# Cosine attention and a gated feed-forward on one core: other load order, batch 2 prepared beside the first output, first output tile ahead of each gate step, loads on the SP queue

## The chip, the cores and the metric

The kernel runs on one core of a Trainium2 chip. The core has a matrix engine (PE; its weight loads are listed as PEld), a vector engine (DVE), an activation engine (ACT), a general engine (POOL) and a queue engine (SP) that only starts transfers. Each engine works through its own list of instructions in order and waits on semaphores. Transfers started by SP go through a hardware queue, those started by POOL through a software queue; both use the same 16 DMA engines. The metric is the device time of one execution in microseconds; the kernel before took 351.66 us, the median of 13 runs (349.85 to 354.13).

## The reference

```
q, k, v: 8 batches x 8 heads x 576 positions x 64, float32
phi(x) = concat(relu(x) * cos(theta_s), relu(x) * sin(theta_s))     theta_s = pi/2 * s / 576
kv  = phi(k)^T v  per batch and head;   z = sum over s of phi(k)
attn = (phi(q) kv) / (phi(q) z + 1e-6)
x   = attn, heads side by side: 4608 tokens x 512
xn  = x / sqrt(mean(x*x) + 1e-6) * rms_g
out = (silu(xn w_gate) * (xn w_val)) w_out        d_ff = 1536
```

The attention is linear: per batch there is one small matrix kv (with z beside it) and a product with it for each position.

## The kernel before, in words

**Tiles.** Of a batch's 576 positions 512 are "main", four tiles (j = 0 to 3) of 128 positions. The other 64 are the rest; the rests of two batches make one more tile (index 4, `NJ`), which is worked on with the odd batch of the pair. The feed-forward goes by blocks of 512 tokens: blocks 0 to 7 are the mains of batches 0 to 7, block 8 holds all rests. d_ff is cut into 12 columns of 128 (`NNT`), so a block has 12 gate steps.

**Attention of one batch b.** `k_prep` (L154) makes phi(k) with two scaled relus, cosine and sine half; `v_prep` (L163) casts v; `kvz` (L217) multiplies them on PE, 40 small matmuls, and `kvz_out` (L231) copies the result to SBUF. `q_scale` (L178) makes phi(q) and `q_tr` (L184) transposes it by a DMA on SP, or `q_tr_pe` and `q_out` do so on PE with a copy. Then, per tile, `nd` (L241): eight matmuls for numerators and denominators; `x_of` (L260): three DVE instructions (den, rec, xt), a Square with a sum on ACT (scr) and a power on POOL (rs); `xn_scale` (L290): the RMS norm on DVE; and the transpose of the result into xnT, by PE and an ACT copy (`xn_tr_pe`, `xn_out`) for batches 0 to 2, by a DMA on SP (`xn_tr`) later. `nd` and `kvz` use one PSUM buffer (pool "att", one deep).

**Feed-forward of one block.** A gate step (`gval`, L351) is eight matmuls 512 wide into two PSUM tiles (four with w_gate, four with w_val), a Silu on ACT (sil) and a product on DVE (hT). Each of the two PSUM tiles has two buffers, so gate step n needs that hT of step n - 2 is done. `outp(blk, i, n)` (L374) does n of the block's 48 output matmuls (four tiles of 12); a tile's last one is followed by `store`: a copy on ACT and a transfer by SP.

**Order.** The order is written out by hand, the same for all engines. Batch 0 comes first. Then gate block 0 (loop at L600) with batch 1's q and k prepared between its steps; then the output of block 0 as a stage of its own (loop at L621, four matmuls a step, all four tiles at once in the PSUM buffers of the gate), with the attention of batch 1 between. From block 1 on (loop at L647) each gate step of block blk is followed by four output matmuls of block blk - 1 (none in block 1), with the next batches' attention around it: `before(b, r)` is what is issued ahead of the gate step, `after(b, r)` what follows, where r counts the gate steps of block b - 1: r = 0 is its first step, negative r lie in block b - 2. Which piece goes to which r stands in `PLAN`, and in `PLAN_2` and `PLAN_3` for batches 2 and 3. After block 8 the output of block 8 follows as the tail.

**Loads.** q, k and v of batch 0 go through SP, everything else through POOL's queue: the six weight pieces of `load_wgv` (512 columns of w_gate and of w_val each), batch 1, `load_wout`, batch 2; from batch 3 on `loads_of` (L510) issues pieces between the gate steps, also on POOL. `raw` tiles have six buffers, taken in the order of the loads: a batch uses those of the batch two before. POOL also computes rs, in the same in-order list. DMAs that POOL or SP issue share eight semaphores per queue in turn, so that a DMA is issued only when the one eight before it has landed.

Of the kernel before, what the change touches and what calls it, by code (L numbers as in the profile page):

```python
# [17 lines left out]
def kernel(  # L18
# [14 lines left out]
    nc = tc.nc  # L33
# [57 lines left out]
    raws = {}  # L91

# [21 lines left out]
    def load(what, src, b):  # L114
        load_piece(what, src, b, 0, H, nc.gpsimd)
        if b % 2 == 0:
            load_rest(what, src, b, nc.gpsimd)
            load_rest(what, src, b + 1, nc.gpsimd)
# [281 lines left out]
    for s in range(0, DFF, 512):  # L400
        load_wgv(s)
# [137 lines left out]
    def plans(t, **pre):  # L539
# [16 lines left out]
    def before(b, r):  # L556
# [4 lines left out]
        for what, n in PLANS.get(b, PLAN)[0].get(r, ()):  # L561
            if n == NJ and what != "v" and b % 2 == (what in ("q", "k")):
                continue
            if what == "q":
                if n == NJ:
                    qr_prep(b)
                else:
                    q_scale(b, n, V, sin_eng)
                    q_tr(b, n)
            elif what == "k":  # L570
                k_prep(b, n, V, sin_eng)
            elif what == "v":
                v_prep(b, n)
            elif what == "kvz_out":
                kvz_out(b, 0, A)
                kvz_out(b, 1, V)
            elif what == "x":
# [5 lines left out]
        if b == 2 and 8 <= r <= 11:  # L583
            xn_out(2, r - 8)

    def after(b, r):
# [3 lines left out]
        for what, n in PLANS.get(b, PLAN)[1].get(r, ()):  # L590
            if what == "kvz":
                kvz(b, 0, H)
            elif n < NJ or b % 2 == 1:
                nd(b, n)
        if b == 2 and 7 <= r <= 10:
            xn_tr_pe(2, r - 7)
# [3 lines left out]
    for nn in range(2, NNT):  # L600
        if 8 <= nn <= 11:
            q_out(1, nn - 8, V if nn % 2 else A)
        if 6 <= nn <= 9:
            q_scale(1, nn - 6, V, A)
        if nn == 9:
            k_prep(1, 0, V, A)
        if nn == 10:
            k_prep(1, 1, V, A)
            qr_prep(0)
        if nn == 11:  # L610
            k_prep(1, 2, V, A)
            k_prep(1, 3, V, A)
        gval(0, nn)
        if 7 <= nn <= 10:
            q_tr_pe(1, nn - 7)
    k_prep(1, NJ, V, A)
    for c in range(NJ + 1):
        v_prep(1, c, A if c % 2 else V)
    for j in range(NJ):
        accs[0, j] = pools["gv"].tile([P, DM], FP32, name="acc", tag="gv"[j % 2])  # L620
    for nn in range(NNT):  # L621
        if nn == 2:
            kvz_out(1, 0, A)
            kvz_out(1, 1, V)
        if 3 <= nn <= 6:
            x_of(1, nn - 3)
        if 5 <= nn <= 8:
            xn_scale(1, nn - 5)
        if 7 <= nn <= 10:
            xn_out(1, nn - 7)  # L630
        for j in range(NJ):
            nc.tensor.matmul(  # L632
                accs[0, j][:, :], lhsT=hTs[0][:, nn, j * P : (j + 1) * P], rhs=wo[:, nn, :],
                start=(nn == 0), stop=(nn == NNT - 1),
            )
        if nn == 1:
            kvz(1, 0, H)
        if 2 <= nn <= 5:
            nd(1, nn - 2)
        if 6 <= nn <= 9:  # L640
            xn_tr_pe(1, nn - 6)
    for j in range(NJ):
        store(0, j, accs[0, j])

    for blk in range(1, NBLK):  # L647
        for nn in range(NNT):
# [49 lines left out]
```

## Time and profile before

| what | us |
|---|---|
| median of 13 runs | 351.66 |
| the profiled execution's own time | 352.21 |
| its span, first to last instruction | 350.4 |
| PE busy | 319.8 |
| DVE, ACT, POOL busy | 193.6, 154.2, 90.9 |

The span cut into 40 slices, with each engine's busy share in tenths, the granted PE clock and the DMA engines:

```profile
PE   1559998988799997999999999999999999999993
DVE  4764475555697795479547974783573322222200
ACT  4634592794545435244534363553443233232221
PEclk9999999999999998999999999999999999999998
DMA  7899999391597999449998999892022001100023
```

A slice is 8.76 us. The first slices are the prologue with batch 0. Gate block 0 ends at 51.6 us, the output of block 0 at 68.2, gate block 1 at 99.5, gate block 2 at 136.2; the tail begins at 333.9. Busy time of PE is counted from the start of a matmul to its modelled end, so groups with a gap between them count 0.17 us more than those without.

### The profile page before, as it was taken

How to read it: one execution, taken by the hardware profiler on the slowest of the kernel's cores; microseconds unless marked ns; L12 is line 12 of the kernel's file. 1: busy time of each engine (PE TensorE's matmuls, PEld its weight loads, DVE VectorE, ACT ScalarE, POOL GpSimd, SP SyncE). 2: the span in 40 equal slices, each digit the busy share in tenths (PEclk: the TensorE clock that was granted, in tenths of full speed). 3: DMA queues.
4: the chain of work that ended last, by engine and by line, in shares of the span. 5: the costliest groups of instructions: out<-in, count | busy, mean ns of one | idle time of the engine just before them, and what ended most of it. 6: DMA issues, size and time to landing. Idle time of an engine off the chain costs nothing.

```text
span 350.4 us, 5676 instructions
## 1 busy us (share of the span) xinstructions
PE 319.8 (91%) x2096; PEld 160.6 (46%) x2096; DVE 193.6 (55%) x419; ACT 154.2 (44%) x304; POOL 90.9 (26%) x135
## 2 busy tenths in 40 slices
PE   1559998988799997999999999999999999999993
PEld 1448454434345543554454445445544444444441
DVE  4764475555697795479547974783573322222200
ACT  4634592794545435244534363553443233232221
POOL 0527622401414572048015711510110000000000
PEclk9999999999999998999999999999999999999998
DMA  7899999391597999449998999892022001100023
GB/s 241 214 206 290 326 303 283 123 278 24 179 181 144 214 183 290 121 103 211 215 101 225 229 173 220 159 257 60 33 74 62 30 30 53 39 30 32 32 60 91
DMA packets 64477, 53.59 MB, mean 153 GB/s; under 512 B 45953, under 2 KB 53633, under 8 KB 64449
## 3 DMA queue, kind: packets, MB, share of 16 engines
q1 hardware_dynamic: 52304, 23.60, 32.7%
q0 software_dynamic: 12144, 29.63, 32.1%
q8 instruction: 16, 0.26, 0.3%
q14 instruction: 13, 0.10, 0.1%
HBM read 38.01 MB, written 9.44 MB: 135 GB/s over the span
## 4 chain that ended last, share of the span: by engine, by line
PE 77%; DVE 8%; ACT 6%; DMA 4%; issue 2%; POOL 0%; SPq 0%; ACTq 0%; DVEq 0%
PE gps L340 23%; PE vps L340 23%; PE acc L377 22%; PE kvz L225 3%; PE nd L254 3%; DVE xt L272 2%; DMA raw<-in_v_dram 2%; DVE hT L349 2%; PE tps L196 1%; ACT sil L348 1%; PE acc L632 1%; DMA raw<-in_q_dram 1%; DMA remk<-in_k_dram 1%; DVE kp L141 1%; ACT scr L280 1%
## 5 line engine op out<-in xcount | busy, mean ns | idle before, releaser
L349 DVE TENSOR_TENSOR hT<-vps,sil 128x512 bf16<-128x512 f32 x108 | 74.4, 690 | 113.8 <-PE vps L340 73.6
L340 PE MATMUL gps<-xnT,wg 128*128 128x512 bf16 (+1 forms) x456 | 113.5, 373 | 2.6 <-ACT sil L348 2.5
L340 PE MATMUL vps<-xnT,wv 128*128 128x512 bf16 (+1 forms) x456 | 113.8, 373 | 0.0
L377 PE MATMUL acc<-wo,hT 128*128 128x512 bf16 x384 | 97.0, 380 | 0.0
L348 ACT ACTIVATE sil<-gps 128x512 bf16<-128x512 f32 x108 | 63.9, 593 | 61.3 <-PE gps L340 58.8
L340 PEld LDWEIGHTS <-wv 128*128 128x128 bf16 x456 | 44.7, 100 | 50.7 <-issue 1.1
L340 PEld LDWEIGHTS <-wg 128*128 128x128 bf16 x456 | 42.1, 100 | 43.9 <-issue 3.6
L285 POOL TENSOR_TENSOR rs<-ssq,mhalf 128x1 f32<-128x1 f32 x36 | 20.5, 570 | 148.3 <-ACT scr L280 148.3
L377 PEld LDWEIGHTS <-hT 128*128 128x128 bf16 x384 | 37.7, 98 | 46.0 <-issue 1.1
L280 ACT ACTIVATE scr<-xt 128x513 bf16<-128x513 f32 x36 | 22.9, 635 | 59.6 <-DVE xt L272 59.6
L359 ACT COPY osb<-acc 128x512 f32<-128x512 f32 x36 | 20.7, 586 | 28.8 <-PE acc L377 28.3
L293 DVE SCALAR_TENSOR_TENSOR xn<-xt,rs,gb 128x512 bf16<-128x512 f32 x36 | 26.7, 743 | 1.3 <-POOL rs L285 1.3
L272 DVE TENSOR_TENSOR xt<-nd,rec 128x512 f32<-128x512 f32 x36 | 24.9, 692 | 1.2
L148 ACT CAST vv<-raw 128x512 bf16<-128x512 f32 x28 | 15.9, 621 | 14.6 <-DMA raw<-in_v_dram 14.6
L254 PE MATMUL nd<-kvzs,qpT 128*128 128x65 bf16 x256 | 14.3, 200 | 5.9 <-DVE xt L272 5.4
L254 PEld LDWEIGHTS <-qpT 128*128 128x128 bf16 x256 | 12.4, 102 | 14.9 <-DVE xt L272 6.2
L141 DVE TENSOR_SCALAR qp<-raw,cos_tab 128x512 bf16<-128x512 f32 x32 | 16.2, 517 | 3.6 <-DMA raw<-in_q_dram 3.6
L225 PE MATMUL kvz<-vv,kp 128*128 128x65 bf16 x256 | 12.4, 199 | 4.7 <-DVE vv L150 3.2
L225 PEld LDWEIGHTS <-kp 128*128 128x128 bf16 x320 | 12.0, 101 | 8.9 <-ACT kp L139 3.4
L97 POOL DMA_DIRECT2D raw<-in_k_dram x20 | 15.3, 764 | 2.6 <-DMA raw<-in_v_dram 2.1
L97 POOL DMA_DIRECT2D raw<-in_v_dram x20 | 15.3, 765 | 2.2 <-DVE qp L141 2.2
L97 POOL DMA_DIRECT2D raw<-in_q_dram x20 | 15.7, 788 | 0.2 <-issue 0.2
(64 smaller groups left out, 190.4 us busy)
## 6 DMA issues: line engine op xcount, KB each, us to landing
out_dram<-osb SPq DMA_DIRECT2D x32, 256.0 KB, 3.2
raw<-in_q_dram POOLq DMA_DIRECT2D x16, 256.0 KB, 7.8
raw<-in_k_dram POOLq DMA_DIRECT2D x16, 256.0 KB, 4.0
raw<-in_v_dram POOLq DMA_DIRECT2D x16, 256.0 KB, 4.9
raw<-in_q_dram POOLq DMA_DIRECT2D x2, 1024.0 KB, 11.2
raw<-in_k_dram POOLq DMA_DIRECT2D x2, 1024.0 KB, 11.1
raw<-in_v_dram POOLq DMA_DIRECT2D x2, 1024.0 KB, 10.7
wg<-in_moe_w_gate_dram POOLq DMA_DIRECT2D x3, 512.0 KB, 9.0
```

The lines of the kernel that those rows point to most:

```text
L97: eng.dma_start(out=raws[what, b][:, h0 : h0 + n, :], in_=src[b, h0 : h0 + n, 0:SM, :].rearrange("h (p j) d -> p h (j d)", j=NJ),)
L225: nc.tensor.matmul(kvz_ps[b][:, h // 2 % 2, c0 : c0 + DE], lhsT=kp[:, c, h, :], rhs=vv[:, c, h, :] if c < NJ else vvr[:, b % 2, h, :], sta ...
L254: nc.tensor.matmul(ps[rows, h // HH, (h % HH) * DE : (h % HH + 1) * DE], lhsT=src[:, h, cols], rhs=kz[:, h, :], start=True, stop=True,)
L272: nc.vector.tensor_tensor(out=xt[:, 0:DM].rearrange("p (g h d) -> p g h d", g=2, d=D), in0=ndv[:, :, :, 0:D], in1=rec[:, :].rearrange("p ( ...
L280: nc.scalar.activation(out=scr[:, :], in_=xt[:, :], func=AF.Square, scale=DM**-0.5, accum_out=ssq[:, :],)
L285: nc.gpsimd.tensor_tensor(out=rs[:, :], in0=ssq[:, :], in1=mhalf[:, :], op=ALU.pow)
L293: nc.vector.scalar_tensor_tensor(out=t[:, :], in0=xt[:, 0:DM], scalar=rs[:, 0:1], in1=gb[:, :], op0=ALU.mult, op1=ALU.mult,)
L340: nc.tensor.matmul(ps[:, c0 : c0 + n], lhsT=w[:, dt, nn * P : (nn + 1) * P], rhs=xnTs[blk][:, dt, c0 : c0 + n], start=(dt == 0), stop=(dt ...
L348: nc.scalar.activation(out=sil[:, :], in_=gps[:, :], func=AF.Silu)
L349: nc.vector.tensor_tensor(out=hTs[blk][:, nn, :], in0=vps[:, :], in1=sil[:, :], op=ALU.mult)
L359: nc.scalar.copy(out=osb[:, :], in_=acc[:, :])
L377: nc.tensor.matmul(acc[:, :], lhsT=hTs[blk][:, nn, j * P : (j + 1) * P], rhs=wo[:, nn, :], start=(nn == 0), stop=(nn == NNT - 1),)
```

## The change

It has five parts.

1. Loads at the start: q and k of batch 1 are put on POOL's queue ahead of the last third of the gate and value weights; after those come v of batch 1, the rests, and w_out's thirds with batch 2's k, v and q between them. `load` becomes `load_first`.
2. Batch 1 is prepared earlier in gate block 0: its q from step 3, its k and v complete before the block's end, and `kvz(1)` ahead of the output of block 0.
3. The output of block 0: its first 8 columns for all tiles at once as before, then the last 4 columns tile by tile, so that the tiles end one after another, with copies by ACT and DVE in turn. The attention of batch 1 takes every second step. Batch 2's k is prepared here, and the rest of batch 2 is spread over block 1 with one tile per two gate steps. Its fourth tile is finished in block 2.
4. From block 2 on, the first output tile (12 matmuls; in block 2, 18) comes ahead of the block's first gate step, and the others are spread over the 12 steps.
5. q, k and v loads from batch 3 on are issued by SP, two gate steps earlier from batch 4 on; the plans of batch 3 (one step later) and of v (from r = -1) are shifted.

```diff
-    def load(what, src, b):
-        load_piece(what, src, b, 0, H, nc.gpsimd)
-        if b % 2 == 0:
-            load_rest(what, src, b, nc.gpsimd)
-            load_rest(what, src, b + 1, nc.gpsimd)
+    def load_first(what, b):
+        load_piece(what, srcs[what], b, 0, H, nc.gpsimd)
+        if b == 2:
+            load_rest(what, srcs[what], 2, nc.gpsimd)
+            load_rest(what, srcs[what], 3, nc.gpsimd)
...
-    def store(blk, j, acc):
+    def store(blk, j, acc, eng=nc.scalar):
         osb = osb_pool.tile([P, DM], FP32, name="osb", tag="osb")
-        nc.scalar.copy(out=osb[:, :], in_=acc[:, :])
+        copy(eng, osb[:, :], acc[:, :])
...
-    for s in range(0, DFF, 512):
-        load_wgv(s)
+    load_wgv(0)
+    load_wgv(512)
+    load_first("q", 1)
+    load_first("k", 1)
...
-    for what, src in (("q", q), ("k", k), ("v", v)):
-        load(what, src, 1)
-        if what == "q":
-            load_rest(what, src, 0, nc.gpsimd)
-        load_rest(what, src, 1, nc.gpsimd)
-    for s in range(3):
-        load_wout(s)
-    for what, src in (("q", q), ("k", k), ("v", v)):
-        load(what, src, 2)
+    load_wgv(1024)
+    load_rest("k", k, 1, nc.gpsimd)
+    load_first("v", 1)
+    load_rest("v", v, 1, nc.gpsimd)
+    load_rest("q", q, 0, nc.gpsimd)
+    load_rest("q", q, 1, nc.gpsimd)
+    load_wout(0)
+    load_first("k", 2)
+    load_wout(1)
+    load_first("v", 2)
+    load_wout(2)
+    load_first("q", 2)
...
-        first, cut = {2: (None, 1), 3: (-9, 2)}.get(b, (-14, 4))
+        first, cut = {2: (None, 1), 3: (-9, 2)}.get(b, (-16, 4))
...
-        load_piece(what, src, b, n * e, n, nc.gpsimd)
+        load_piece(what, src, b, n * e, n, nc.sync)
         if e == cut - 1 and b % 2 == 0:
-            load_rest(what, src, b, nc.gpsimd)
-            load_rest(what, src, b + 1, nc.gpsimd)
+            load_rest(what, src, b, nc.sync)
+            load_rest(what, src, b + 1, nc.sync)
...
     PLAN = plans(
-        1, q=each(-5, 5), k=each(-3, 5), v=((-2, (0, 1)), (-1, (2, 3)), (0, (4,))),
+        1, q=each(-5, 5), k=each(-3, 5), v=((-1, (0, 1)), (0, (2, 3, 4))),
     )
     PLAN_3 = plans(
-        2, q=each(-2, 5), k=((-1, (0,)), (0, (1, 2)), (1, (3,)), (2, (4,))),
-        v=((0, (0, 1)), (1, (2, 3)), (2, (4,))),
-    )
-    PLAN_2 = plans(
-        4, q=((0, (0, 1)), (1, (2, 3))), k=((2, (0, 1)), (3, (2, 3)), (4, (4,))),
-        v=((2, (0, 1)), (3, (2, 3)), (4, (4,))),
+        3, q=each(0, 4), k=((0, (0, 1)), (1, (2,)), (2, (3,))),
+        v=((1, (0, 1)), (2, (2, 3, 4))),
+    )
+    PLAN_2 = plan_of(
+        k=[(-9, (0,)), (-7, (1,)), (-5, (2,)), (-3, (3,)), (-1, (4,))],
+        v=[(0, range(NJ + 1))], kvz_out=[(2, (0,))],
+        q=[(2, (0, 1)), (3, (2, 3))],
+        x=[(5, (0,)), (7, (1,)), (9, (2,)), (11, (3,))],
+        xn=[(6, (0,)), (8, (1,)), (10, (2,))],
+        xn_out=[(8, (0,)), (10, (1,))],
+    ), plan_of(
+        kvz=[(1, (0,))], nd=[(4, (0,)), (6, (1,)), (8, (2,)), (10, (3,))],
+        xn_tr=[(7, (0,)), (9, (1,)), (11, (2,))],
     )
...
     for nn in range(2, NNT):
-        if 8 <= nn <= 11:
-            q_out(1, nn - 8, V if nn % 2 else A)
+        if 5 <= nn <= 8:
+            q_out(1, nn - 5, V if nn % 2 else A)
+        if 3 <= nn <= 6:
+            q_scale(1, nn - 3, V, A)
         if 6 <= nn <= 9:
-            q_scale(1, nn - 6, V, A)
+            k_prep(1, nn - 6, V, A)
         if nn == 9:
-            k_prep(1, 0, V, A)
+            k_prep(1, NJ, V, A)
         if nn == 10:
-            k_prep(1, 1, V, A)
-            qr_prep(0)
+            v_prep(1, 0, A)
+            v_prep(1, 1, V)
+            v_prep(1, 2, A)
         if nn == 11:
-            k_prep(1, 2, V, A)
-            k_prep(1, 3, V, A)
+            v_prep(1, 3, V)
+            v_prep(1, NJ, V)
         gval(0, nn)
...
+    kvz(1, 0, H)
...
-        for j in range(NJ):
+        if nn == 11:
+            qr_prep(0)
+        if nn in (5, 7, 9, 11):
+            xn_out(1, nn // 2 - 2)
+        before(2, nn - 12)
+        for j, m in ((j, nn) if nn < 8 else (nn - 8, 8 + j) for j in range(NJ)):
...
+        if nn >= 8:
+            store(0, nn - 8, accs[0, nn - 8], V if nn % 2 else A)
...
+            if blk == 2 and nn == 0:
+                xn_scale(2, 3)
+                xn_out(2, 2)
             for b, r in ahead:
                 before(b, r)
+            first = {1: 0, 2: NNT + 6}.get(blk, NNT)
+            if blk >= 2 and nn == 0:
+                outp(blk - 1, 0, NNT)
+                if blk == 2:
+                    xn_tr_pe(2, 3)
+                    xn_out(2, 3)
+                outp(blk - 1, NNT, first - NNT)
             gval_mm(blk, nn, 0, SM)
             gval_end(blk, nn)
             if blk >= 2:
-                outp(blk - 1, 4 * nn, 4)
+                i, e = (first + (NJ * NNT - first) * m // NNT for m in (nn, nn + 1))
+                outp(blk - 1, i, e - i)
```

More of the change, by code (lines that the diff above doesn't have):

```diff
@@ L91 @@
     raws = {}
+    srcs = {"q": q, "k": k, "v": v}
     def load_piece(what, src, b, h0, n, eng):
@@ L572, in before @@
             elif what == "v":
-                v_prep(b, n)
+                v_prep(b, n, V if b == 2 and n % 2 else A)
             elif what == "kvz_out":
@@ L576, in before @@
                 kvz_out(b, 1, V)
+            elif what == "xn_out":
+                xn_out(b, n)
             elif what == "x":
@@ L582, in before @@
                 xn(b, n)
-        if b == 2 and 8 <= r <= 11:
-            xn_out(2, r - 8)
     def after(b, r):
@@ L592, in after @@
                 kvz(b, 0, H)
+            elif what == "xn_tr":
+                xn_tr_pe(b, n)
             elif n < NJ or b % 2 == 1:
                 nd(b, n)
-        if b == 2 and 7 <= r <= 10:
-            xn_tr_pe(2, r - 7)
     for nn in range(2, NNT):
-        if 8 <= nn <= 11:
-            q_out(1, nn - 8, V if nn % 2 else A)
+        if 5 <= nn <= 8:
+            q_out(1, nn - 5, V if nn % 2 else A)
+        if 3 <= nn <= 6:
+            q_scale(1, nn - 3, V, A)
         if 6 <= nn <= 9:
-            q_scale(1, nn - 6, V, A)
+            k_prep(1, nn - 6, V, A)
         if nn == 9:
-            k_prep(1, 0, V, A)
+            k_prep(1, NJ, V, A)
         if nn == 10:
-            k_prep(1, 1, V, A)
-            qr_prep(0)
+            v_prep(1, 0, A)
+            v_prep(1, 1, V)
+            v_prep(1, 2, A)
         if nn == 11:
-            k_prep(1, 2, V, A)
-            k_prep(1, 3, V, A)
+            v_prep(1, 3, V)
+            v_prep(1, NJ, V)
         gval(0, nn)
[L614 to L618, printed above, removed]
+        if 4 <= nn <= 7:
+            q_tr_pe(1, nn - 4)
+    kvz(1, 0, H)
     for j in range(NJ):
@@ L621 @@
     for nn in range(NNT):
-        if nn == 2:
+        if nn == 0:
             kvz_out(1, 0, A)
             kvz_out(1, 1, V)
[L625 to L630, printed above, removed]
-        for j in range(NJ):
+        if nn in (1, 3, 5, 7):
+            x_of(1, nn // 2)
+        if nn in (4, 6, 8, 10):
+            xn_scale(1, nn // 2 - 2)
+        if nn == 11:
[4 more added lines that the diff above has]
+        for j, m in ((j, nn) if nn < 8 else (nn - 8, 8 + j) for j in range(NJ)):
             nc.tensor.matmul(
-                accs[0, j][:, :], lhsT=hTs[0][:, nn, j * P : (j + 1) * P], rhs=wo[:, nn, :],
-                start=(nn == 0), stop=(nn == NNT - 1),
-            )
[L636 to L643, printed above, removed]
+                accs[0, j][:, :], lhsT=hTs[0][:, m, j * P : (j + 1) * P], rhs=wo[:, m, :],
+                start=(m == 0), stop=(m == NNT - 1),
+            )
+        if nn >= 8:
+            store(0, nn - 8, accs[0, nn - 8], V if nn % 2 else A)
+        if nn in (0, 2, 4, 6):
+            nd(1, nn // 2)
+        if nn in (4, 6, 8, 10):
+            xn_tr_pe(1, nn // 2 - 2)
     for blk in range(1, NBLK):
```

## The prediction

> **What bounds the kernel now.** I read the page first, then PE's busy time stage by stage, then PE's list of waits, and last the timelines of the places that this list names.
>
> ```profile
> span 350.4 us, 5676 instructions
> PE 319.8 (91%) x2096; PEld 160.6 (46%) x2096; DVE 193.6 (55%) x419; ACT 154.2 (44%) x304; POOL 90.9 (26%) x135
> ```
>
> PE is the bound, and the instruction lists of both kernels hold the same 4194 rows for PE: only PE's idle and slow time can go. The stages below are the stage of output 0 (with batch 1), gate block 1 (with batch 2), gate block 2 (with batch 3), the first step of block 3, and the rest up to the last output.
>
> ```profile
> 51.59:68.16 16.57, 14.82 (x138) 7.55 (x137) 10.86 (x26) 7.81 (x19) 6.51 (x8) 1.00 0.63 191
> 68.16:99.46 31.30, 25.50 (x185) 12.32 (x184) 18.64 (x39) 20.96 (x43) 6.75 (x10) 1.00 0.61 180
> 99.46:136.19 36.73, 34.77 (x250) 17.13 (x249) 28.25 (x64) 15.65 (x35) 18.18 (x26) 1.00 0.95 192
> 136.19:140.46 4.27, 4.27 (x12) 1.59 (x12) 4.27 (x10) 3.05 (x6) 0.00 (x0) 0.60 1.11 293
> 140.46:333.88 193.42, 193.42 (x1170) 92.80 (x1169) 101.82 (x200) 75.34 (x149) 37.16 (x55) 1.00 0.52 112
> ```
>
> Columns: stretch, its length, busy us of PE, PEld, DVE, ACT, POOL, granted clock, DMA share, GB/s. From 140.46 on PE has no gap: nothing can be gained there, only lost. The prologue (0 to 32.5 us) and the tail keep their order. So the whole case is the stretch 51.6 to 140.5. Who makes PE wait in it:
>
> ```profile
> PE gps L340 <- ACT sil L348: 2.5, 2, 2.0
> PE nd L254 <- DVE xt L272: 2.4, 5, 0.9
> PE tpx L314 <- DVE xn L293: 2.0, 3, 1.4
> PE kvz L225 <- ACT vvr L170: 1.5, 1, 1.5
> ```
>
> The waits on xt and xn are one loop through the in-order engines:
>
> ```profile
> 90.81 0.64 ACT L280 ACTIVATE scr<-xt 128x513 bf16<-128x513 f32 x1 [1.88 <-DVE xt L272]
> 91.91 0.60 ACT L348 ACTIVATE sil<-gps 128x512 bf16<-128x512 f32 x1
> 92.54 0.69 DVE L349 TENSOR_TENSOR hT<-vps,sil 128x512 bf16<-128x512 f32 x1 [1.18 <-ACT sil L348]
> 93.58 0.69 DVE L272 TENSOR_TENSOR xt<-nd,rec 128x512 f32<-128x512 f32 x1
> 94.19 0.74 DVE L293 SCALAR_TENSOR_TENSOR xn<-xt,rs,gb 128x512 bf16<-128x512 f32 x1
> 94.99 0.40 PE L314 MATMUL tpx<-ident,xn 128*128 128x128 bf16 x4 [1.45 <-DVE xn L293]
> ```
>
> The Square (scr) of one tile stands ahead of the gate's Silu on ACT, hT behind that on DVE, the next xt behind hT, and PE's transpose behind xn: 3.1 us a round (scr at 87.73, then 90.81), while PE has 2.2 us of work in it. The 2.0 us wait on sil is a load:
>
> ```profile
> 127.35 0.60 ACT L348 ACTIVATE sil<-gps 128x512 bf16<-128x512 f32 x1
> 134.50 1.14 ACT L148 CAST vv<-raw 128x512 bf16<-128x512 f32 x2 [6.55 <-DMA raw<-in_v_dram]
> 135.55 0.59 ACT L348 ACTIVATE sil<-gps 128x512 bf16<-128x512 f32 x1
> ```
>
> ACT stands 6.55 us on batch 4's v pieces with a Silu queued behind; PE idles 1.96 us and then runs at half clock.
>
> **What the Trainium skill says.** "TensorE: Matmul & The Clock Gate", Part 1 (the HAM clock gate): a low-activity window of about 3.4 us halves PE's clock. The trace agrees on the length (0.5 for 3.41 us from 136.61) but shows that 1.96 us of idling was enough; 1.53 us at 79.7 was not. "DMA: Bandwidth & Descriptors", Issuing engines are not separate DMA queues: another issuer moves no bytes faster, it saves issue time only. Here an issue costs POOL 0.75 us and SP 0.47. The same page, Queues, rings and completion order: a DMA engine takes turns between rings, packet by packet. The trace fits: where POOL's loads and SP's transposes ran together, four transposes landed a median 13.7 us after issue (160 to 176), and 3.9 us where only one load was beside them (229 to 238).
>
> **The change, part by part.** Unit prices from starts: four 512-wide matmuls 0.862, a gate step (eight) 1.725, kvz 1.21, nd 0.26, tpx 0.24 on PE; on DVE hT 0.60, the three of x_of 1.05, xn 0.66, a q or k pair 0.79, a cos half 0.40; on ACT sil 0.5 to 0.6, scr with its read 0.72, a sin half 0.62, xnT 0.57.
>
> *Loads ahead of the last weights.* POOL's issues show the pace:
>
> ```profile
> 35.65 1.50 POOL L130 DMA_DIRECT2D wo<-in_moe_w_out_dram  x2 [1.40 <-DMA raw<-in_q_dram]
> 41.95 1.05 POOL L97 DMA_DIRECT2D raw<-in_k_dram  x1 [1.58 <-DMA raw<-in_v_dram]
> 44.79 0.69 POOL L109 DMA_DIRECT2D remk<-in_k_dram  x1 [1.11 <-DMA wo<-in_moe_w_out_dram]
> ```
>
> Each issue waits until the DMA eight earlier has landed. A full 1 MB load takes about 2.57 us in turn (landings 30.2, 32.8, 35.4 in the trace), a rest 0.4, weights as much as q. Six such loads end at 32.8 as before, now q1 and k1 in the last two places. In the new order the last weights land at about 37.9, v1 40.9, wo 44.6 / 50.4 / 56.4, k2 47.1, v2 53.0, q2 58.9. First uses: gate step 8 at 44.5, v1 at 48, wo at 53 / 57 / 62, k2 at 57, v2 at 67, q2 at 72. Smallest margin 5.5 us: cost 0, gain 0 here. If the cover were gone (the queue 8 us late), wo's last third would stop PE for 2 to 3 us and halve the clock after it, 4 us in all. rs on POOL is not blocked: its last load issue falls near 49, the first rs of batch 1 at 56.
>
> *Gate block 0.* The q1 transposes move from steps 7..10 to 4..7; PE work is the same, end 51.6. v1's last copies now stand on DVE before hT(11): vvr ends near 52.0, kvz(1) waits 0.4.
>
> *Output 0.* PE: 48 matmuls 10.35, kvz 1.21, four nd 1.04, four tpx 0.96 = 13.55 us. Before it took 16.57. Added on DVE per pair of steps: x_of 1.05, a k2 cos half 0.40, xn 0.66 = 2.1 us, against PE's 2.2: nearly level, and xn stands behind the k half, so that a tpx waits 0.45 three times or so, 0.75 the last time (an output copy on DVE, estimated at 0.65 by the PSUM-reading hT, stands ahead of its xn). With 0.25 at the first nd and 0.3 at vvr and xnT: 2.2 us of waits, 15.8 us in all: **-0.75 us**. Bounds: -2.5 (no wait) to +1 (DVE lags two whole rounds).
>
> *Gate block 1.* Batch 2's k is done by now, its tiles come every second step: PE 3.95 us a round against DVE's 2 x 0.60 + 1.05 + 0.66 = 2.9 and the chain's 3.1. The ACT pile-up at the head (four output copies, sines, v) is cut too. PE: 12 x 1.725 + 1.21 + 1.04 + 3 x 0.24 = 23.7, against 31.30 before: **-7.55 us**, taking 0.1 for the first nd. That nd reads transposes issued some 3 us before it; they landed 2.8 to 4.9 us after issue here: 0 to 1.2 us is possible.
>
> *Gate block 2.* Its first gate step now follows 18 output matmuls (3.9 us), which hide xn, tpx and xnT of tile 3. Batch 3's chain moves one step later (x at steps 5 to 9), over batch 4's q and k (from step 7): DVE needs 3.1, 3.1, 3.9, 2.8 us in steps 7 to 10, while a step of PE is 2.27 (2.53 with nd). DVE falls about 2.5 us behind; the two gate buffers absorb 1.2. I get 0.6 us at nd of tile 4, 0.9 at gate step 11, 0.3 at the first output of block 3. v4's last piece is issued at r = -5 and first copied at -1, four steps of 2.3 us later, before that two of them: the 1.96 us wait goes, and the half clock with it (the twelve matmuls of the row 136.19:140.46 took 4.27 us and take 2.59 at full clock, 0.17 more went in the group after: 1.85). So 36.73 becomes 36.1 (**-0.6**), the clock **-1.85**, the later wait **+0.3**.
>
> *Loads on SP.* Per two blocks SP gets 24 issues at 0.47 and six rests at 0.8, 8 us per block; it now spends some 20 of 34 on transposes and stores. Behind each stand transposes and stores.
>
> ```profile
> 161.70 6.48 SPq L186 DMA_TRANSPOSE qpT<-qp  x2
> 168.91 12.96 SPq L186 DMA_TRANSPOSE qpT<-qp  x2
> ```
>
> These four were slow beside POOL's loads; the second landed at 182.0 and was read at 183.0. One ring in turn (about 1.1 us a transpose, 0.7 a piece) should land them sooner. Bounds: nothing gained, as PE has no gap there, to several us a batch if a load holds the queue. I take 0. The first output tile ahead of each gate step moves 12 matmuls and adds none: 0.
>
> Sum: 0.75 + 7.55 + 0.6 + 1.85 - 0.3 = 10.45 us. The profiled execution took 352.21 (span 350.4 and 1.8 around it); less 10.45 is 341.8. It stands 0.55 above the median 351.66, so the median becomes **341.2 us**.
>
> **Rivals.**
> 1. *The waits change their name* (DVE's rounds, or the qpT transposes): block 1 keeps about 2 us, block 2 its 2 us at the old or new place, output 0 gains nothing. For it: DVE is level with PE in output 0 and over it in late block 2. Against: the spacing gives 3.95 us to a 3.1 us chain. Gain about 5.5: 346.
> 2. *Everything goes*: the 2.2 and 1.8 us that I leave do not appear, or more than half of them does not: 338.7. For it: small slips are usually absorbed; against: the DVE sums above.
> 3. *SP's one queue in order* (slower). A load held for its buffer or lane holds qpT behind it; that tile had 1 us of margin. If each of the batches 3 to 7 comes 3.5 us later than now, PE idles 2.5 and runs 3.4 us at half clock (1.7): 4.2 x 5 = 21, 362. It decides from 2.1 us per batch on. Against: a buffer is free nine steps or more before its load is issued, and POOL's ring no longer takes turns with the transposes.
> 4. *It does not do what it says*: a weight or v piece is still late once: 4 us back, 345.
>
> **How the numbers follow.** Forecast 0.58 (own range 339.6 to 343.2), rival 1 0.19, rival 2 0.13, rival 3 0.06, rival 4 0.04. The range takes in rivals 1, 2 and 4 nearly whole: 338.2 to 346.3. About 0.3% (1 us) is what can be told from no change. Faster 0.92, same 0.02 (taken from rival 1's far end), slower 0.06.
>
> **What would show it.** Right: block 1 under 25 us; no wait of ACT on v; clock 1.00 from 31 us to the tail; output 0 about 15 to 16 us with waits of tpx on xn; small waits on DVE at the end of block 2; qpT landing under 8 us after issue. Wrong: a new PE gap after 140 us, waits of nd on qpT's DMA, gate step 8 of block 0 or the output waiting for weights, or a half-clock stretch in the middle.

## The result and the profile after

The changed kernel takes 343.0 us (median of 11 runs, 341.87 to 344.12). The kernel before took 352.03 in the same comparison (48 runs). The ratio is 0.9748 with a 95% interval of 0.9725 to 0.9771: 9.0 us less, where 10.45 were forecast. The forecast of 341.2 us had a range of 339.6 to 343.2, and 343.0 lies just inside its upper end. In the experiments below, one execution of 679.07 us (of four of e2_sp_only) and one of 352.64 us (of twenty of e1_pool) were slow, over 1.5% above the fastest of their kernel, and are left out of the medians.

The page of the changed kernel, its span and the busy time of each engine:

```profile
span 341.3 us, 5669 instructions
PE 315.8 (93%) x2096; PEld 159.3 (47%) x2096; DVE 193.6 (57%) x423; ACT 152.5 (45%) x300; POOL 40.7 (12%) x69
```

PE has the same 2096 matmuls. POOL lost more than half of its busy time, because it no longer issues the loads from batch 3 on; PE waited for POOL in neither kernel. What counts is where PE stood still or ran slowly. The same stages as before, one row each (stretch, length, busy us of PE, PEld, DVE, ACT, POOL, granted clock, DMA share, GB/s), from the start of the output of block 0 on:

```profile
51.41:66.89 15.48, 14.21 (x138) 7.74 (x136) 11.45 (x27) 8.80 (x20) 2.27 (x4) 1.00 0.61 183
66.89:90.71 23.82, 23.79 (x181) 12.35 (x180) 15.63 (x33) 13.72 (x28) 1.64 (x3) 1.00 0.77 234
90.71:127.43 36.72, 35.33 (x254) 17.18 (x252) 30.12 (x69) 18.41 (x40) 4.06 (x7) 1.00 0.80 175
127.43:133.04 5.61, 4.71 (x23) 2.03 (x21) 4.39 (x11) 3.43 (x6) 0.00 (x0) 1.00 0.94 213
133.04:325.29 192.25, 191.89 (x1162) 91.86 (x1161) 100.53 (x201) 75.12 (x148) 9.89 (x18) 1.00 0.45 117
```

Gate block 1, the second row, went from 31.30 to 23.82 us, and PE's busy time fills it. The output of block 0 went from 16.57 to 15.48. Gate block 2 takes 36.72, as it did. The row with a clock of 0.60 has gone: the clock is 1.00 in every row. The fourth row holds 23 matmuls where the row of before held 12, so the two are not to be compared by length.

To compare whole kernels I use the *middle*: from the first 512-wide gate matmul of block 0 to the first output matmul of block 8. It leaves out the prologue, whose length changes from run to run (last section). The middle was 302.04 us (32.54 to 334.58) and is 293.58 (32.36 to 325.94): 8.46 less. The span fell by 9.2 us; the rest of this is 0.18 in the prologue and 0.55 after the last matmul, both in places where the change moves nothing.

The 8.46 are made up of: output 0, -1.09; gate block 1, -7.48; the half clock that no longer follows, -1.68 (twelve matmuls took 4.27 us, and 2.59 at full clock); +0.5 in later blocks, where two of the periods from a block's first gate matmul to the next block's are 34.21 us and were 33.96; and, as the remainder, +1.3 in gate block 2 with the start of block 3.

These figures are of one traced execution each, and the half clock is not in every execution of the kernel before. Of 54 others whose clock is on record, 25 had a mean granted clock of 0.996 or more, which leaves no room for 3.41 us at half clock (that alone takes 0.005 from the mean over 350 us). Their median is 350.44 us. The eight at 0.988 to 0.992 have room for one or two such stretches, and their median is 352.39. So in a comparison of medians the term counts only in part.

PE's list of waits in the changed stretch (engine, line, awaited instruction; us in total, times, longest):

```profile
PE tpx L315 <- DVE xn L294: 1.5, 4, 0.6
PE acc L378 <- DVE hT L350: 1.5, 2, 0.9
PE nd L255 <- DVE xt L273: 0.5, 1, 0.5
```

The 2.5 us on sil and the 1.5 on vvr are gone, and what waits are left all end on DVE. The second line is new. One of its two waits, 0.57 us, is at the head of gate block 2, and the timeline shows how it comes about (start, length, instruction, in brackets the idle time before it and what ended it):

```profile
90.01 0.68 DVE L350 TENSOR_TENSOR hT<-vps,sil 128x512 bf16<-128x512 f32 x1
...
91.04 0.69 DVE L273 TENSOR_TENSOR xt<-nd,rec 128x512 f32<-128x512 f32 x1
91.82 0.64 ACT L281 ACTIVATE scr<-xt 128x513 bf16<-128x513 f32 x1 [2.13 <-DVE xt L273]
...
92.45 0.58 ACT L349 ACTIVATE sil<-gps 128x512 bf16<-128x512 f32 x1
...
93.07 0.69 DVE L350 TENSOR_TENSOR hT<-vps,sil 128x512 bf16<-128x512 f32 x1 [1.33 <-ACT sil L349]
...
93.81 0.39 PE L378 MATMUL acc<-wo,hT 128*128 128x512 bf16 x1 [0.57 <-DVE hT L350]
```

It is the loop of before once more. The fourth tile's xt stands behind hT of gate step 10 on DVE; ACT's Square waits for it with the last Silu of the block queued behind; DVE stands 1.33 us for the Silu; and the twelfth matmul of the output needs the hT that follows.

### The profile page after: what moved, and what is told of

Same layout as the page of the kernel before. It is cut to its first block, busy times and chain, and to the rows that moved or that the text cites. A ratio compares the mean times of both kernels' runs of the same rounds, so it can differ in the third digit from the quotient of the medians.

```text
span 341.3 us, 5669 instructions
## 1 busy us (share of the span) xinstructions
PE 315.8 (93%) x2096; PEld 159.3 (47%) x2096; DVE 193.6 (57%) x423; ACT 152.5 (45%) x300; POOL 40.7 (12%) x69
## 4 chain that ended last, share of the span: by engine, by line
PE 79%; DVE 12%; ACT 3%; issue 2%; DMA 2%; SPq 0%; DVEq 0%; ACTq 0%
PE gps L341 24%; PE vps L341 24%; PE acc L378 20%; PE kvz L226 3%; DVE hT L350 3%; DVE xt L273 3%; PE nd L255 3%; DVE xn L294 2%; DVE kp L142 2%; DMA raw<-in_q_dram 2%; PE acc L649 2%; PE tps L197 1%; ACT scr L281 1%; ACT sil L349 1%; DVE rec L270 1%
## 5 line engine op out<-in xcount | busy, mean ns | idle before, releaser
L341 PE MATMUL vps<-xnT,wv 128*128 128x512 bf16 (+1 forms) x456 | 112.4, 370 | 0.0
L378 PE MATMUL acc<-wo,hT 128*128 128x512 bf16 x384 | 97.3, 379 | 1.5 <-DVE hT L350 1.5
L341 PEld LDWEIGHTS <-wg 128*128 128x128 bf16 x456 | 41.7, 99 | 40.8 <-issue 0.2
L149 ACT COPY osb<-acc 128x512 f32<-128x512 f32 x34 | 19.9, 585 | 25.4 <-PE acc L378 23.4
L255 PEld LDWEIGHTS <-qpT 128*128 128x128 bf16 x256 | 12.6, 102 | 11.5 <-DVE xt L273 3.6
L142 DVE TENSOR_SCALAR qp<-raw,cos_tab 128x512 bf16<-128x512 f32 x32 | 15.2, 486 | 4.4 <-DMA raw<-in_q_dram 4.4
L149 ACT CAST vv<-raw 128x512 bf16<-128x512 f32 x26 | 14.8, 620 | 2.6 <-DMA raw<-in_v_dram 2.6
L142 DVE TENSOR_SCALAR kp<-raw,cos_tab 128x512 bf16<-128x512 f32 x32 | 15.2, 482 | 0.0
L197 PE MATMUL tps<-ident,qp 128*128 128x128 bf16 x64 | 6.3, 264 | 8.6 <-ACT qp L140 8.4
L649 PE MATMUL acc<-wo,hT 128*128 128x512 bf16 x48 | 11.5, 379 | 0.0
```

Of the source, the lines that this page charges most:

```text
L142: nc.vector.tensor_scalar(out=dst, in0=src, scalar1=tab[lanes, col : col + 1], scalar2=0.0, op0=ALU.mult, op1=ALU.max,)
L149: nc.scalar.copy(out=dst, in_=src)
L255: nc.tensor.matmul(ps[rows, h // HH, (h % HH) * DE : (h % HH + 1) * DE], lhsT=src[:, h, cols], rhs=kz[:, h, :], start=True, stop=True,)
L341: nc.tensor.matmul(ps[:, c0 : c0 + n], lhsT=w[:, dt, nn * P : (nn + 1) * P], rhs=xnTs[blk][:, dt, c0 : c0 + n], start=(dt == 0), stop=(dt ...
L378: nc.tensor.matmul(acc[:, :], lhsT=hTs[blk][:, nn, j * P : (j + 1) * P], rhs=wo[:, nn, :], start=(nn == 0), stop=(nn == NNT - 1),)
```

## The experiments

All times are medians. "Middle" is that of the profiled execution, with the half clock that this one execution happened to have.

| run | against | us | ratio (95%) | middle |
|---|---|---|---|---|
| the kernel before | | 352.03 | 1 | 302.04 |
| the changed kernel | | 343.0 | 0.9748 (0.9725 to 0.9771) | 293.58 |
| e1_pool | after | 349.75 | 0.996 (0.994 to 0.9981) | 299.78 |
| e2_sp_only | before | 364.62 | 1.0389 (1.0321 to 1.0456) | 318.49 |
| e8_part5 | before | 348.09 | 0.9894 (0.9848 to 0.994) | 298.16 |
| e3_each_step | after | 344.88 | 0.9815 (0.9767 to 0.9863) | 295.35 |
| e4_old_order | after | 343.09 | 0.9762 (0.9716 to 0.9808) | 293.61 |
| e10_first0 | after | 344.94 | 0.9818 (0.978 to 0.9857) | 296.99 |
| e5_first8 | after | 342.36 | 0.9737 (0.9696 to 0.9778) | 293.18 |
| e6_sin_act | after | 343.6 | 0.9763 (0.9725 to 0.98) | 294.24 |
| e7_both | after | 342.97 | 0.9753 (0.9715 to 0.9792) | 293.84 |
| e9_plan3 | after | 343.12 | 0.9778 (0.9737 to 0.9819) | 293.81 |
| e11_plan3_first8 | after | 342.72 | 0.9753 (0.972 to 0.9787) | 293.07 |
| e12_plan3_late_q | after | 343.27 | 0.9748 (0.9698 to 0.9798) | no value |

"Against" names the kernel that was edited; every ratio is to the kernel before. The trace of e12_plan3_late_q lacks some matmul records, so its middle can't be read.

### Which queue: the loads on POOL again, or on SP alone

e1_pool takes the changed kernel and gives the loads from batch 3 on back to POOL, at their new places:

```diff
-        load_piece(what, src, b, n * e, n, nc.sync)
+        load_piece(what, src, b, n * e, n, nc.gpsimd)
```

(The rests likewise.)

> The changed kernel with the loads from batch 3 on given back to POOL; their earlier places stay. Theory (the earlier issue of v is what ends the wait on it, the SP queue adds nothing on PE's path): ACT waits less than 1 us on v of batch 4, no half clock near 130 us, 342.5 to 344; the qpT transposes go back from a mean landing of 3.5 us to 8 or more. Rival (the queue does it): ACT waits 3 to 6 us on v4, PE idles about 2 us and runs 3.4 us at half clock: 346 to 347.

It loses 6.2 us of middle, and not where either theory had looked. v of batch 4 comes in time (ACT's list has no wait on it): its earlier places see to that, on either queue. What comes late is qpT of batch 3. The timeline of PE in e1_pool:

```profile
118.48 0.62 PE L255 MATMUL nd<-kvzs,qpT 128*128 128x65 bf16 x8 [4.29 <-DMA qpT<-qp]
118.92 1.90 PE L341 MATMUL gps<-xnT,wg 128*128 128x512 bf16 x4
```

PE stands 4.29 us for a transpose of q, and the group after it takes 1.90 us for the work of 1.03: from 117.4 to 124.2 the clock is 0.50. The transposes issued from 100 to 117 us, by the view of DMA issues (last number: median us from issue to landing), first in e1_pool and then in the changed kernel:

```profile
qpT<-qp SPq DMA_TRANSPOSE x3, 11.7
```

```profile
qpT<-qp SPq DMA_TRANSPOSE x3, 4.5
```

The transposes are issued by SP in both. Beside loads in the software queue they take 11.7 us, and 4.5 in one queue with them. So SP's queue is worth 6.2 us in the new plan (6.8 by medians). About 2.8 of them are the half clock that the wait brings: an estimate, half of the 5.7 us that PE worked from 117.4 to 124.2.

e2_sp_only makes the same edit the other way round: the kernel before, with nothing changed but that SP issues these loads, at the old places.

> The kernel before with the loads from batch 3 on given to SP, at their old places, nothing else. Theory (issue place decides): v4's last piece is still issued about 127 to 128 us and first used at 128, so ACT waits 2.5 us or more on it; PE idles 0 to 1 us because transfers in one ring land some 3 us sooner: 348 to 351.5. Rival (the queue does it): no wait of PE and no half clock there, 3.8 us off: 347.5 to 348.5. Third: SP's order holds transposes back and it is slower than 352.

It is 3.9% slower than before, 13.7 us by the ratio; the traced execution (366.98 us) is the slowest of three. ACT's and PE's timelines around batch 4's v:

```profile
137.61 1.14 ACT L148 CAST vv<-raw 128x512 bf16<-128x512 f32 x2 [9.49 <-DMA remv<-in_v_dram]
```

```profile
139.29 1.87 PE L340 MATMUL gps<-xnT,wg 128*128 128x512 bf16 x4 [4.90 <-ACT sil L348]
```

and SP's own timeline, where the length is the time that the issue took:

```profile
129.29 2.06 SPq L362 DMA_DIRECT2D out_dram<-osb  x1
131.40 0.43 SPq L97 DMA_DIRECT2D raw<-in_v_dram  x1
131.92 1.19 SPq L308 DMA_TRANSPOSE xnT<-xn  x1
133.21 1.25 SPq L186 DMA_TRANSPOSE qpT<-qp  x1
134.52 0.58 SPq L97 DMA_DIRECT2D raw<-in_v_dram  x1
```

Between two pieces of v, SP issues two transposes, 2.4 us together; the last piece is issued at 134.52, where POOL issued it at 127.80 in the kernel before. It lands 2.9 us later, at 137.45, which is quick: before, it took 6.6 us. (The bracket names remv, but remv lands after the cast has begun; it is the last piece of raw that ends the wait.) The transfer isn't slow: its issue is late, because in SP's in-order list it stands behind transposes and stores. These take time to issue, and in part they wait for their own sources: 7.5 us of waits in SP's list from 117 to 138 us. ACT then waits 9.49 us with the Silus behind it. After 100 us PE stands 12.6 us on Silus in four waits, and three of the four bring a half clock. (A fourth half clock of this execution, from 79.81 us, has nothing to do with these loads; see the last section.) This is the forecast's rival of the one queue in order, with the loads in the queue's way turned round: not the load holds the transposes, they hold the load.

e8_part5 gives the kernel before the whole of the fifth part but batch 3's shift: SP's queue, the loads two gate steps earlier, and v from r = -1.

```diff
-        first, cut = {2: (None, 1), 3: (-9, 2)}.get(b, (-14, 4))
+        first, cut = {2: (None, 1), 3: (-9, 2)}.get(b, (-16, 4))
...
-        1, q=each(-5, 5), k=each(-3, 5), v=((-2, (0, 1)), (-1, (2, 3)), (0, (4,))),
+        1, q=each(-5, 5), k=each(-3, 5), v=((-1, (0, 1)), (0, (2, 3, 4))),
```

(And `nc.gpsimd` to `nc.sync`, as above.)

> The kernel before with part 5 of the change nearly whole: loads from batch 3 on by SP, two gate steps earlier from batch 4 on, v from batch 4 on used from r = -1; plans of batches 2 and 3, load order and output as before. Theory (the queue needs the earlier places, and both together end the late v): no wait of PE on a Silu behind v, no half clock, 3.8 us off, 347 to 348.5. Rival (SP's order holds v back whatever its place): waits on v in several batches as with the queue alone, over 352.

The middle is 3.88 us shorter than before, with no late v and no half clock. Against e2_sp_only it is 20.3 us (16.5 by medians): two gate steps of earlier issue and one step of later use together decide what SP's queue is worth. Which of the two does it wasn't tried. Without SP (e1_pool) the other edits bring 2.26 us, the fifth part nearly whole 3.88, and all together 8.46, so the parts need each other. From first gate matmul to first gate matmul, block 1 takes 29.28 us in e1_pool as in the changed kernel, and block 2 takes 41.04 in place of 35.14: what block 1 gains is lost in block 2 if batch 3's transposes come late.

### Which loop: batch 2's tiles every step

e3_each_step leaves everything but the distance of batch 2's tiles in block 1: one per gate step instead of one per two.

```diff
-        x=[(5, (0,)), (7, (1,)), (9, (2,)), (11, (3,))],
+        x=[(5, (0,)), (6, (1,)), (7, (2,)), (8, (3,))],
...
-        kvz=[(1, (0,))], nd=[(4, (0,)), (6, (1,)), (8, (2,)), (10, (3,))],
+        kvz=[(1, (0,))], nd=[(4, (0,)), (5, (1,)), (6, (2,)), (7, (3,))],
```

(xn, xn_tr and xn_out follow in the same way.)

> The changed kernel with batch 2's chain (nd, x, xn and PE transpose) in block 1 at every gate step again, as before the change, and batch 2's k still prepared in the output stage. Theory (the loop of 3.1 us a round through scr, sil, hT, xt and xn is what block 1 paid): block 1 rises from 23.8 to 26.5 to 28 us; the head of block 2 loses its waits of 1.3 us, as tile 3 is finished earlier; 344 to 346. Rival (the pile of ACT work at the head of block 1 was the cost, not the spacing): block 1 stays under 25 us and the time is 342 to 343.

Gate block 1's row, and one of the two waits in it:

```profile
67.34:93.70 26.36, 24.39 (x182) 12.15 (x181) 16.86 (x35) 15.22 (x32) 2.19 (x4) 1.00 0.79 239
```

```profile
82.39 0.42 PE L255 MATMUL nd<-kvzs,qpT 128*128 128x65 bf16 x8 [0.91 <-DVE xt L273]
```

The block takes 26.36 us instead of 23.82, and nd waits 0.91 and 0.94 us for xt, so the rounds are those 3.1 us of Square, Silu, hT and xt again (from 82.39 to 85.47, the starts of the two nd that wait). In return the wait on hT at the head of block 2 is gone, since the fourth tile is done earlier. Of 2.54 us lost, 1.77 remain in the middle.

The distance is thus worth 2.5 of the 7.5 us that block 1 gained. The waits of PE in block 1 of the kernel before show where the others lay:

```profile
PE tpx L314 <- DVE xn L293: 2.0, 3, 1.4
PE kvz L225 <- ACT vvr L170: 1.5, 1, 1.5
PE nd L254 <- DVE xt L272: 1.3, 2, 0.9
PE gps L340 <- ACT sil L348: 0.6, 1, 0.6
PE kvz L225 <- ACT vv L148: 0.3, 1, 0.3
```

2.4 us of these waits are on v's copies and a Silu, ahead of the tiles. They stay away in e3_each_step, and so do the 2.0 on xn. Batch 2's k in the stage before, its v shared with DVE, and the later finish of the fourth tile are in both kernels; no run takes these apart.

### What the load order at the start is worth

e4_old_order puts the last third of the gate weights ahead of batch 1's q and k again.

```diff
     load_wgv(512)
-    load_first("q", 1)
-    load_first("k", 1)
+    load_wgv(1024)
...
-    load_wgv(1024)
+    load_first("q", 1)
+    load_first("k", 1)
```

> The changed kernel with the last third of the gate and value weights again ahead of q and k of batch 1; all else as changed. Theory (margins of 4 us and more): q1 lands at 35.4 us, first used near 34.5 ahead of the Silu of gate step 3, so ACT and DVE wait about 1 us once and PE at most 0.5 us: 343 to 343.7. Rival (part 1 is needed by the earlier preparation): PE waits 1.5 us or more in gate block 0: 344.5 to 346.

The middle is 293.61 against 293.58. q of batch 1 lands at 35.8, DVE waits 1.28 us for it, and PE doesn't wait. This part of the change brings nothing by itself, and costs nothing.

### The first output tile ahead of the gate step

e10_first0 issues no output matmul ahead of the gate steps from block 3 on; e5_first8 issues 8 instead of 12.

```diff
-            first = {1: 0, 2: NNT + 6}.get(blk, NNT)
+            first = {1: 0, 2: NNT + 6}.get(blk, 0)
```

(8 in place of 0 in the second; the calls of `outp` are adapted.)

> The changed kernel without the first output tile ahead of the gate step from block 3 on (in block 2 it stays). Theory (in block 3 those 12 matmuls cover the last xnT transpose, later they cover nothing): the first gate step of block 3 waits 2 to 2.8 us on the transpose of xnT, no other block waits; 344 to 344.8. Rival (they only ask for hT too early and cover nothing): 341.7 to 342.6.

> The changed kernel with 8 instead of 12 output matmuls ahead of the first gate step from block 3 on. Theory (the wait of 1.3 us at the first output tile of block 3 comes only from asking for the last hT column too early): that wait goes, 341.5 to 342.3. Rival (DVE is behind, so the wait moves into the first gate steps of block 3): 342.7 to 343.3.

The first gate step of block 3 in e10_first0:

```profile
130.53 1.02 PE L341 MATMUL gps<-xnT,wg 128*128 128x512 bf16 x4 [3.17 <-DMA xnT<-xn]
```

It waits 3.17 us for the transpose of x, and the clock is 0.50 from 131.6 to 135.0: 3.4 us of middle in all. This execution (346.03 us) is the slowest of four; two of the others had a mean clock of 0.998, which leaves no room for that half clock, and by medians the part is worth 1.9 us. In the blocks after it PE's list has no such wait, and the periods are 33.96 and 33.32 us, as in the kernel before, where the changed kernel has 34.21 and 33.32. So the part covers one transfer, in one block, and is also what costs the 0.5 us in the later ones. Of e5_first8 PE's list from 120 to 135 us has one line:

```profile
PE gps L341 <- DMA xnT<-xn: 0.9, 1, 0.9
```

With 8 matmuls the 0.90 us on hT at 131.09 turn into 0.92 on the transpose at 129.95. The later periods are 34.0 us instead of 34.21. The middle is 0.4 shorter, but the intervals of the two ratios overlap widely; by time the two can't be told apart.

### Where the load of block 2 can go

The other runs try to remove the waits that the changed kernel has in gate block 2. e6_sin_act gives the sine halves of batch 4 to ACT, e7_both adds the 8 matmuls of e5_first8:

```diff
-        sin_eng = A if b == 2 else V
+        sin_eng = A if b in (2, 4) else V
```

> The changed kernel with the sine halves of batch 4's q and k on ACT, 0.40 us less of DVE for each pair and 0.62 more of ACT. Theory (DVE's load in steps 7 to 11 of block 2 makes both late waits): nd of tile 4 waits under 0.3 and the last hT column under 0.4 us, 341.2 to 342. Rival (ACT is full there too and its Silu comes late instead): 342.7 to 344.

> Both of the two last edits together. Theory: no wait over 0.3 us after gate step 1 of block 2, 341 to 341.8, no more than 0.4 under the better of the two alone, since both take away the same wait. Rival: ACT's added work shows as waits on sil, 342.5 or more.

In e6_sin_act the wait on hT at the start of block 3 has gone, and in its place stand 1.12 us at nd of tile 4 and one on a Silu:

```profile
125.89 1.02 PE L341 MATMUL gps<-xnT,wg 128*128 128x512 bf16 x4 [0.93 <-ACT sil L349]
```

The rows from 118 to 127 us, of the changed kernel and of e6_sin_act:

```profile
118.00:127.00 9.00, 8.49 (x53) 3.94 (x52) 8.86 (x22) 5.31 (x12) 1.62 (x3) 1.00 0.95 158
118.00:127.00 9.00, 6.95 (x46) 3.18 (x45) 6.82 (x15) 5.72 (x13) 1.12 (x2) 1.00 1.01 174
```

DVE, busy 8.86 of the 9 us in the changed kernel, has 6.82 here, and ACT 5.72. Neither is full, and PE still waits: in ACT's list a sine half of 0.71 us now stands ahead of the Silu, and hT and xt on DVE wait behind that. e7_both lies between its two halves (293.84).

e9_plan3 gives batch 3 its plan of before, one step earlier; e11_plan3_first8 adds the 8 matmuls; e12_plan3_late_q keeps the earlier chain but prepares q late and in pairs, with the 8 matmuls.

```diff
-        3, q=each(0, 4), k=((0, (0, 1)), (1, (2,)), (2, (3,))),
-        v=((1, (0, 1)), (2, (2, 3, 4))),
+        2, q=each(-2, 5), k=((-1, (0,)), (0, (1, 2)), (1, (3,)), (2, (4,))),
+        v=((0, (0, 1)), (1, (2, 3)), (2, (4,))),
```

> The changed kernel with batch 3's plan as before the change (its chain one step earlier, its q from r = -2, so before the end of block 1). Theory (the step later is what piles batch 3's chain on batch 4's q and k): nd of tile 4 waits under 0.3 us and the last hT column of block 2 under 0.6, against 0.5 and 0.9 in the list of waits; 341.7 to 342.6. Rival (the pile only moves to the head of block 2, where q of batch 3 now stands on DVE ahead of tile 3's chain): the waits there grow by 0.8 us or more and the time is 342.9 to 344.

> Batch 3's earlier plan with 8 matmuls ahead of the first gate step from block 3 on. Theory (earlier chain, so xnT lands before it is asked for): no wait over 0.3 us after the head of block 2, 341 to 342. Rival (head of block 2 pays it back): 342.5 to 344.

> Batch 3's products and chain one step earlier, as before the change, but its q prepared in steps 0 and 1 of block 2 and v in steps 1 and 2, so that the end of block 1 has none of it; 8 matmuls ahead of the first gate step from block 3 on. Theory (the waits of the changed kernel in block 2 come from DVE's order alone): head of block 2 as in the changed kernel (0.6 and 0.3 us in the list of waits), up to 0.5 at gate step 3, nothing later: 341.2 to 342.2. Rival (DVE in steps 0 to 2 is the new place, or the q transposes land too late for nd at step 3): 343 or more.

In e9_plan3 the waits at the end shrink to under 0.3 us, and the one at the head grows from 0.57:

```profile
94.00 0.39 PE L378 MATMUL acc<-wo,hT 128*128 128x512 bf16 x1 [1.51 <-DVE hT L350]
```

In e12_plan3_late_q the head is at 0.57 again, the end stays under 0.3, and a third place opens, where kvz waits for k on DVE:

```profile
105.30 0.20 PE L226 MATMUL kvz<-vv,kp 128*128 128x65 bf16 x1 [1.71 <-DVE kp L142]
```

e11_plan3_first8 has the shortest middle, 293.07. None of these six can be told from the changed kernel by its ratio. The times of all but e5_first8 fell where their rivals had put them. DVE is 82% busy in gate block 2 (30.12 of 36.72), and in each of the other five the waits move instead of going. What would take work from DVE there without giving it to ACT, batch 4's q and k later still, wasn't tried.

## Why the prediction was right, step by step

**Gate block 1** (-7.55 forecast, -7.48 measured) was right in size, and its reason is shown in part. e3_each_step brings the 3.1 us rounds back, and with them 2.54 us. That k's earlier place and the emptier head of the block bring the rest, as the step said, fits the waits that are gone, but no run shows it by itself. The first nd, for which 0.1 was taken, waits for nothing: its transpose landed at 75.93 and it starts at 76.73.

**The half clock** (-1.85 forecast, -1.68 measured): it is gone because v of batch 4 comes in time, as the step said. e8_part5 and e1_pool show that the earlier issue and the later use together do it, whichever the queue. That the whole 1.85 was counted is right for the profiled execution only, as many executions of the kernel before have no half clock there; the forecast of the median took this out again in part, with the 0.55 between the two. ACT still waits for v, 2.6 us in three waits, the longest 1.2, and PE doesn't notice.

**Output 0** (-0.75 forecast, -1.09 measured): the tpx waits came as forecast in kind, 0.29, 0.33 and 0.58. The 0.4 at kvz, forecast for gate block 0, didn't come.

**Loads at the start** (0): right. The landings were 37.8, 40.8 and 44.6 / 50.6 / 56.4 for the weights, v and w_out, within 0.2 us of the forecast, and q of batch 2 came at 59.6 instead of 58.9. e4_old_order shows that the order gains nothing.

**Gate block 2 and the start of block 3** (-0.6 and +0.3 forecast, +1.3 measured) is the term that was mis-sized, by 1.6 us, and with the +0.5 of the later blocks it makes up more than the whole difference to the forecast of 10.45; output 0 gives 0.3 back. The failing step is that the first gate step "now follows 18 output matmuls (3.9 us), which hide xn, tpx and xnT of tile 3". After eleven of them the twelfth needs hT of gate step 11, and that hT stands behind the same tile's Square. The prediction had counted no round of the loop for this last tile. This costs 0.57 at hT and 0.27 at tpx, 1.3 us of PE with the gaps that the list leaves out (5.46 us from 90.71 to the first gate matmul, for 4.12 of work). The other waits of the step came, in other places than named: nd of tile 4 0.51 (0.6 forecast), gate step 11 none (0.9 forecast), the start of block 3 0.90 by the list and 1.07 by the starts of the matmuls (0.3 forecast). The DVE backlog was real, and came out one step later than I had put it.

**Loads on SP** (0): right in the sum, wrong as a price. Taken by itself in the new plan the queue is worth 6.2 us of middle, because PE would have a gap without it: at qpT of batch 3, which the change itself moves later. I had looked for late transposes only from 140 us on, in a kernel whose batch 3 was still at the old place. With the loads at the old places, the same edit costs 16.5 us of middle in the traced execution, 13.7 by the ratio. The bounds ran from nothing to several us a batch, and the runs show both ends; that 0 came out right was luck of the earlier issue and the later use. The transposes after 108 us landed in 3.5 us on the mean, 5.0 at most; before it was 8.8 and 18.5. After 140 us the sooner landings gain nothing, since PE had no gap there.

**The first tile ahead** (0): it is worth 3.4 us once, in block 3 (e10_first0; 1.9 by medians), by covering the transposed x. Against the kernel before that is no gain, since that kernel had no wait on a transfer there; the +0.5 of the later blocks is its price, which was left out.

The rival of the renamed waits was half true: in block 2, not in block 1.

## What to carry to other kernels

A chain that goes through in-order engines has a round time of its own (3.1 us here); give its turns a distance longer than that, and look at the last turn, which meets the next stage's first need. When loads are moved to another queue, price what stands ahead of each issue in that queue's list, not the transfer: the same edit was worth 6.8 us with earlier issues and later use, and cost 13.7 without (by medians and ratio). Where five plans only move a wait, look at all engines of the chain: taking work from the busiest one, and giving it to the next, moved the wait as well.

## What the hardware showed that was not expected

**A short wait can halve the clock, and it matters where it falls.** In the kernel before 1.96 us of idling was followed by 3.41 us at 0.5. A wait of 3.17 us (e10_first0) was followed by one such stretch, one of 4.29 us (e1_pool) by two, 6.8 us. Waits of 1.51 (e9_plan3) and 1.71 us (e12_plan3_late_q) were followed by none. The length alone doesn't decide. The wait for vvr in block 1 is the same in the kernel before, in e8_part5 and in e2_sp_only, here of the last:

```profile
78.45 0.19 PE L225 MATMUL kvz<-vvr,kp 128*128 128x65 bf16 x1 [1.53 <-ACT vvr L170]
```

Only in e2_sp_only a half clock follows, from 79.81 to 83.22.

In each of the 14 traces, all changes of the clock lie whole multiples of 3.413 us apart: in the kernel before 31 of them lie between 30.80, where full clock begins, and 136.61. I divided the 13 complete traces into stretches of this length, counted from that beginning, and added up PE's idle time in each of the 1176 stretches. Of those at full clock, all six with 1.96 us or more were followed by half clock, and none with 1.74 or less. Between them one with 1.79 was followed by it (the one just shown, from 76.39 us), and one with 1.93 was not (e2_sp_only, from 250.47 us). So something over half of such a stretch has to be idle. A wait of 2 us halves the clock only if nearly all of it falls into one stretch, which would explain why many executions of the kernel before have no half clock. The Trainium skill, "TensorE: Matmul & The Clock Gate", HAM oscillation, gives the rule as no idle gaps over about 3.4 us; here the measurement decides, and a gap of 2 us was already too long.

**The prologue's length is in good part a matter of the clock.** The first 512-wide gate matmul started anywhere from 31.25 to 33.17 us in the profiled executions of kernels with the same prologue work. The first gate step itself, 128 wide, began at 25.90 to 26.95. The clock is halved for part of the prologue (0.5 from 15.9 to 29.5 us in the changed kernel's execution), and when it comes back differs, from 28.28 to 31.60 us; the matmuls show it too, which start 0.107 us apart before and 0.056 after. From the first gate step to the first 512-wide matmul it took 5.07 us in e1_pool, where the clock came back 1.9 us after that step began, and 6.56 in e7_both, where it came back after 5.0. The same page, Part 1, says that the activity window runs freely and that the ramp varies from run to run, which agrees. The whole is up to 1.9 us, more than any of the six variants of block 2 moves, and the reason for comparing by the middle.

**A DMA transpose suffers beside another queue's loads.** With 2.6 MB moved from 100 to 117 us and loads in the software queue it took 11.7 us to land, and 4.5 with 3.2 MB moved in the same stretch and the loads in its own queue. More bytes, sooner landing. In e2_sp_only, where nothing but the queue of the loads differs from the kernel before, q's transposes after 108 us land in 3.6 us on the mean (4.8 at most), and before it was 8.8 (18.5). That a DMA engine takes turns between rings, as the forecast quoted, would explain it; no run here shows the turns themselves. A rival stands open: in SP's one list a load is issued only after the transposes ahead of it, so fewer loads may be under way beside a transpose.
